# Reordering the last third of a prologue: rims, exps, table load and the third gate group of an attention and gated-FFN kernel

## The chip, the cores and the metric

The kernel runs on one core of a Trainium2 chip. The metric is the device time of one execution in microseconds (us). One core has five engines that matter here: PE (matmuls), ACT (activations and copies), DVE (vector operations), POOL (issues the loads and does some copies) and SP (issues stores and transposing transfers). PE accumulates into PSUM, of which this kernel uses eight banks.

All runs here are recorded as fast. But some runs of some experiments have a mean granted clock (the share of full speed that PE was allowed) of 0.986 to 0.993 instead of 0.997 to 1.0.

## The reference

Attention over 4 batches, 8 heads, 768 positions and 64 dimensions. Each query sees keys nearer than 16 positions, and the maximum (keys) or mean (values) of each 32-position block. Then a gated feed-forward layer on the concatenated heads:

```
scores_l = scale * q @ k.T          # masked to |i-j| < 16
scores_s = scale * q @ blockmax(k).T + log(32)
a = softmax(concat(scores_l, scores_s))
x = a @ concat(v, blockmean(v))     # 3072 tokens x 512
out = x + sigmoid(x @ w_res) * ((gelu(x @ w_gate) * (x @ w_val)) @ w_out)
```

## The kernel before

Work goes in eight units of 384 tokens. A unit has twelve gate and value groups ("fo"): four matmuls of 384 columns for the gate, four for the value, a gelu on ACT, a product on DVE. From the second unit on, the attention of the next unit lies between the matmuls of the current one. The first unit has nothing to hide its attention behind; that is the prologue, and it is written out by hand, in program order per engine.

Terms: a *rim* is a copy of neighbouring value rows into the rows 64 to 95 of a value tile, so that one matmul covers a 64-query tile and its 16 neighbours on each side. Heads go in four pairs. `vsum_pair` is PE's block means of a pair, copied by ACT to `vblk`. `av_band` and `av_blk` multiply the probabilities with the values and with the block means; `av_blk` also normalises on DVE (`rz`, `xn`) and so gives a PSUM bank back. `xt_step` transposes x on PE and copies it to `xT`. `keep_warm` multiplies zeros; it is there for PE's clock (without the last two of these matmuls four of six runs lost the clock, e8 below).

```python
def xt_step(u, ko, st, pool, tag, copy=nc.vector.tensor_copy):
    xp = pool.tile([128, TU], BF16, tag=tag, name="xp")
    # three PE transposes into xp (cut)
    copy(st["xT"][:, ko, :], xp[:])

def gv_end(gvT, fo, g, vv):
    ge = work.tile([128, TU], F32, tag="ge", name="ge")
    nc.scalar.activation(ge[:], g[:, 0:TU], AF.Gelu)
    nc.vector.tensor_mul(gvT[:, fo, :], ge[:], vv[:, 0:TU])

def mm_tile(name):                      # four banks in turn
    return ps_mm.tile([128, 512], F32, tag="mm", name=name)

def keep_warm(n, pool=ps_s, tag="s"):   # ps_s: the two score banks
    wp = pool.tile([128, 2 if pool is ps_s else 1, 512], F32, tag=tag, name="wp")
    for _ in range(n):
        nc.tensor.matmul(wp[:, 0], warm[:, 0:128], warm[:], start=True, stop=True)

# the last third of the prologue
s_step(0, 3, st, MM2, mid=lambda: vsum_pair(1, *o_bank))
pair_rims(1)
keep_warm(1, *t_bank)
av_band(0); av_blk(0)
keep_warm(1, *t_bank)
vsum_pair(2, *t_bank)
pair_rims(2)
pair_rims(3, nc.scalar.copy)
av_band(1); av_blk(1)
keep_warm(1)
vsum_pair(3, *o_bank)
# (cut: pair 2, a warming matmul, transposes and pair 3 in turn, one more warming matmul)
nc.scalar.activation(gate1[:], bias_t[0:1, :], AF.Gelu)   # brings the table load forward
# (cut: gates of groups 0 and 1 slice by slice, values behind them)
```

The softmax here doesn't subtract the row's maximum and nothing guards it: scores larger than these inputs give would overflow.

Of the kernel before, what the change touches and what calls it, by code (L numbers as in the profile page):

```python
# [8 lines left out]
F32 = mybir.dt.float32  # L9
BF16 = mybir.dt.bfloat16  # L10
AF = mybir.ActivationFunctionType
# [4 lines left out]
def kernel(  # L16
# [11 lines left out]
    nc = tc.nc  # L28
    B, H, S, D = q.shape
# [9 lines left out]
    QT = 64  # L39
# [99 lines left out]
    with tc.manual_schedule():  # L139
# [39 lines left out]
        load_q(0, q_sb[0], 1, 2)  # L179
        v_loads(0)  # L180
        load_w(w_gate, wg_src, 0)
        for x in (vext[0], vext[1][:, 0:HT]):
            pad = x[0:QT, :, :, D + 1:VP]
            nc.scalar.activation(pad, warm[0:QT, 0:1].unsqueeze(1).unsqueeze(1).to_broadcast(list(pad.shape)), AF.Copy)
        nc.vector.memset(band[:], 0.0)
# [11 lines left out]
                                    scalar1=-1.0, scalar2=240000.0, op0=ALU.add, op1=ALU.mult)  # L197
        kw_consts(0)
        nc.vector.memset(vblk[96:128, :, D:D + 1], 1.0)
        nc.vector.memset(vext[1][0:QT, HT:NT, :, D + 1:VP], 0.0)  # L200

        for c in range(6):
            if c:
# [70 lines left out]
        def pair_rims(hp, copy=nc.vector.tensor_copy):  # L274
            own_rims(0, HT, False, slice(2 * hp, 2 * hp + 2), copy)
            own_rims(0, HT, True, slice(2 * hp, 2 * hp + 2), copy)

        def vsum_pair(hp, pool, tag):
            vs = pool.tile([128, 512], F32, tag=tag, name="vs")
            hs = slice(2 * hp, 2 * hp + 2)  # L280
            for t in range(NT):
                nc.tensor.matmul(vs[:, 0:2 * D], bmat[:, t:t + 4, :], vext[0][0:QT, t, hs, 0:D],  # L282
                                 start=(t == 0), stop=(t == NT - 1))
            nc.scalar.copy(vblk[96:128, hs, 0:D], vs[96:128, 0:2 * D].rearrange("p (h d) -> p h d", d=D))
# [34 lines left out]
                                     start=(u > 0), stop=True,  # L319
                                     skip_group_check=True)  # L320

        def s_step(u, hp, st, banks=None, tiles=None, mid=None):
            if tiles:
                s, banks = tiles, True
            elif banks:
                s = [p.tile([128, 512], F32, tag=tag, name="s") for p, tag in banks]
            else:
                s2 = ps_s.tile([128, 2, 512], F32, tag="s", name="s")
                s = [s2[:, hh] for hh in range(2)]
            s_mm(u, hp, [x[:, 0:TU] for x in s])  # L330
            if mid:
                mid()
            P = ppool.tile([128, 2, HT, QT], BF16, tag="P", name="P")
            if banks:
                for hh in range(2):
                    nc.scalar.activation(P[:, hh].rearrange("p t q -> p (t q)"), s[hh][:, 0:TU], AF.Exp,  # L336
                                         scale=scale, bias=bias_t[:])
            else:
                nc.scalar.activation(P.rearrange("p a t q -> p a (t q)"), s2[:, :, 0:TU], AF.Exp,  # L339
                                     scale=scale, bias=bias_t[:])  # L340
            if u:
                Pf = P.rearrange("p a t q -> p (a t) q")
                nc.vector.tensor_mul(Pf, Pf, maskt.unsqueeze(1).to_broadcast([128, 2 * HT, QT]))  # L343
            st["P", hp] = P
# [34 lines left out]
        def xt_step(u, ko, st, pool, tag, copy=nc.vector.tensor_copy):  # L379
            xp = pool.tile([128, TU], BF16, tag=tag, name="xp")  # L380
            for sub in range(NSUB):
                nc.tensor.transpose(xp[:, sub * 128:(sub + 1) * 128],  # L382
                                    st["xn"][:, ko, sub, :], ident[:])
            copy(st["xT"][:, ko, :], xp[:])  # L384
# [20 lines left out]
        def mm_tile(name):  # L405
            return ps_mm.tile([128, 512], F32, tag="mm", name=name)
# [67 lines left out]
        def keep_warm(n, pool=ps_s, tag="s"):  # L474
# [3 lines that stand above are left out]
# [18 lines left out]
        def ao_tile(hp):  # L496
            ao[hp] = ps_mm.tile([128, NSUB, 2, D + 1], F32, tag="mm", name="ao")

        def av_band(hp):
            av_first(hp, st, ao[hp], 0, BAND)  # L500

        def av_blk(hp):
            av_first(hp, st, ao[hp], BAND, 128)
            av_end(hp, st, ao[hp])
# [12 lines left out]
        s_step(0, 2, st)  # L517
        keep_warm(2, *o_bank)
        pair_rims(0)
        s_step(0, 3, st, MM2, mid=lambda: vsum_pair(1, *o_bank))  # L520
        pair_rims(1)
        keep_warm(1, *t_bank)
        av_band(0)
        av_blk(0)
        keep_warm(1, *t_bank)
        vsum_pair(2, *t_bank)
        pair_rims(2)
        pair_rims(3, nc.scalar.copy)
        av_band(1)
        av_blk(1)  # L530
        keep_warm(1)
        vsum_pair(3, *o_bank)
        ao_tile(2)
        ao_tile(3)
        av_band(2)
        av_blk(2)
        keep_warm(1)
        xt_step(0, 0, st, **t_turn)
        av_band(3)
        av_blk(3)  # L540
        keep_warm(1)
        xt_step(0, 1, st, **t_turn)
        nc.scalar.activation(gate1[:], bias_t[0:1, :], AF.Gelu)
        g0, v0, g1 = mm_tile("g"), mm_tile("vv"), mm_tile("g")
        gv_mm(g0, w_gate, st, 0, (0, 1))
        xt_step(0, 2, st, ps_o, "ao")
        gv_mm(g1, w_gate, st, 1, (0, 1))
        gv_mm(g0, w_gate, st, 0, (2,))
        gv_mm(g1, w_gate, st, 1, (2,))
        xt_step(0, 3, st, ps_t, "t")  # L550
        gv_mm(v0, w_val, st, 0, (0, 1, 2))
        v1 = mm_tile("vv")
        gv_mm(v1, w_val, st, 1, (0, 1, 2))
        gv_mm(g0, w_gate, st, 0, (3,))
        gv_mm(v0, w_val, st, 0, (3,))
        gv_end(gvT, 0, g0, v0)
        gv_mm(g1, w_gate, st, 1, (3,))
        gv_mm(v1, w_val, st, 1, (3,))
        gv_end(gvT, 1, g1, v1)

        def unit0_extras(fo):
            if fo == 2:
# [89 lines left out]
        for u in range(NU):  # L652
            b, half = u // 2, u % 2
            nb = b + 1
            if half == 0 and nb == 1:
                k_sb[nb] = k_tile()
                load_k(nb, k_sb[nb], 0, 1)
                v_loads(nb)
                load_q_nat(nb)
            if u:  # L660
                gvT = upool.tile([128, FO, TU], BF16, tag="gvT", name="gvT")
            for fo in range(0 if u else 2, FO):
                if u > 1 and fo == 0:
                    fo_first(st, gvT)
                elif u and fo == FO - 2:
                    fo_last_two(st, gvT)
                elif u == 0 or fo < FO - 2:
                    fo_step(st, gvT, fo)
                if u == 0:
                    unit0_extras(fo)  # L670
                if u == 0 and fo == 9:
                    tq = turn_all(q_sb[1])
                if u == 0 and fo in (9, 10):
                    for hp in range(2 * fo - 18, 2 * fo - 16):
                        q_place(1, hp, tq[hp])
                if half == 0 and 1 < nb < B and fo == 0:
                    pool_after(st["xT"][0:1, KO - 1, 0:1])
                    k_nat = load_k_nat(nb)
                    v_loads(nb)
                if half == 0 and b and fo == 1:  # L680
                    v_rims(b, HT, NT)
                if half == 0 and 1 < nb < B and fo == 6:
                    turn_k(nb, k_nat)
                    k_rims(nb, slice(0, NP), nc.gpsimd)
                if half == 1 and nb < B:
                    if fo == 0:
                        v_rims(nb, 0, HT)
                        if nb > 1:
                            pool_after(st["xT"][0:1, KO - 1, 0:1])
                            load_q_nat(nb)  # L690
                    if fo == (5 if nb == 1 else 1):
                        turn_q(nb, 0)
                        turn_q(nb, 1)
                        vsum_grp(nb, ps_t, "t")
                        for i in range(2):
                            vsum_bc(nb, 3 * i, 3 * i + 3, nc.gpsimd)
                    if nb == 1:
                        if fo == 0:
                            tk = turn_all(k_sb[nb])
                        if fo in (0, 2, 4, 6):  # L700
                            hp = (2, 0, 1, 3)[fo // 2]
                            k_place(nb, hp, tk[hp])
                    elif 2 <= fo < 2 + NP:
                        k_blocks(nb, fo - 2)
            if u == NU - 1:
                last_out(u, st, gvT)
            else:
                nst = new_unit()
                (mid_out if u else first_out)(u, st, gvT, nst)
                st = nst  # L710
# [30 lines left out]
```

## Time and profile before

| | before |
|---|---|
| time | 258.07 us median of 4 runs (257.75 to 258.23) |
| span in the profile | 256.1 us |
| PE busy | 247.7 us, 97% |
| last score step starts | 14.63 us |
| third gate group starts | 25.74 us, 11.11 us later |

The difference in the last row, from the first matmul of the last score step to the first of the third gate group, is my ruler below: it contains all that the change does except the split of the pads, which comes earlier, and it is free of the scatter of the other 230 us. The prediction shows the lines on which it rests. Two more from the page of the profile, first its head, then the granted clock in tenths over 40 slices of the span:

```profile
span 256.1 us, 5856 instructions
...
PEclk9999999999999999999999999999999999999999
```

From the timeline (start, length, engine, line, operation): the last score step, the first rim copy of pair 2 on DVE and both of pair 3 on ACT.

```profile
14.63 0.34 PE L310 MATMUL s<-ident,mneg 64*128 64x384 bf16 x2
...
17.60 0.40 DVE L272 COPY vext<-vext 32x640 bf16<-32x640 bf16 x1
...
18.27 0.72 ACT L272 COPY vext<-vext 32x640 bf16<-32x640 bf16 x1
...
19.02 0.83 ACT L269 COPY vext<-vext 16x768 bf16<-16x768 bf16 x1
```

DVE copies pair 2's rims behind the first normalisation (17.01 to 17.57), and ACT is taken by pair 3's rims until 19.85. With those on it, ACT has no idle stretch as long as the 1.28 us of the gelu table between 16.13 and the load at 22.40; its longest is 0.80.

### The profile page before, as it was taken

Reading aid. Unit: us, or ns where it says so; the run is one execution under the profiler, and the core shown is the slowest. Engines: PE = TensorE matmul, PEld = TensorE weight load, DVE = VectorE, ACT = ScalarE, POOL = GpSimd, SP = SyncE. Lnnn points to the kernel's source line nnn. Section 1 sums busy time; section 2 is a strip of 40 time slices with the busy share of each in tenths; the row PEclk is TensorE's granted clock in tenths of the full one; section 3 lists DMA queues with packets and bytes.
Section 4 is the critical chain, followed back from the end, with each engine's and each line's share of the span. In section 5 each row is a group of like instructions: output and inputs, shape, how many; then the busy total and the mean of one; then the engine's idle time right before and its main releaser. Section 6 shows DMA issues by size and latency. Waiting matters only on the chain.

```text
span 256.1 us, 5856 instructions
## 1 busy us (share of the span) xinstructions
PE 247.7 (97%) x2306; PEld 140.0 (55%) x2331; DVE 158.5 (62%) x364; ACT 129.6 (51%) x216; POOL 96.9 (38%) x128
## 2 busy tenths in 40 slices
PE   7999999999999999999999999999999999999994
PEld 2675565565654565545654555546554565556544
DVE  6984785489567544867667544767567544854424
ACT  8775449355583337344493338344482338253320
POOL 8885452360705980255405980365404000000000
PEclk9999999999999999999999999999999999999999
DMA  5999999999403999279603999579703400240003
GB/s 80 176 181 196 197 204 207 174 168 184 99 4 84 192 148 171 43 137 180 125 5 100 177 152 151 67 132 174 127 17 95 117 3 0 48 140 0 4 0 123
DMA packets 98107, 29.34 MB, mean 115 GB/s; under 512 B 83224, under 2 KB 94944, under 8 KB 97984
## 3 DMA queue, kind: packets, MB, share of 16 engines
q0 software_dynamic: 68352, 14.76, 66.3%
q1 hardware_dynamic: 29728, 14.21, 24.7%
q8 instruction: 18, 0.29, 0.5%
q14 instruction: 9, 0.07, 0.1%
HBM read 29.36 MB, written 6.29 MB: 139 GB/s over the span
## 4 chain that ended last, share of the span: by engine, by line
PE 92%; DVE 5%; issue 2%; ACT 0%; DVEq 0%
PE g L397 25%; PE vv L397 24%; PE f L445 23%; PE r L435 8%; PE s L317 3%; PE ao L357 3%; PE vs L282 1%; PE tp L220 1%; PE ao L369 1%; PE vs L290 1%; PE wp L477 1%; DVE ks L237 1%; DVE o L454 1%; DVE th L451 1%; PE xp L382 1%
## 5 line engine op out<-in xcount | busy, mean ns | idle before, releaser
L403 DVE TENSOR_TENSOR gvT<-ge,vv 128x384 bf16<-128x384 f32 x96 | 52.7, 552 | 49.2 <-PE vv L397 45.3
L402 ACT ACTIVATE ge<-g 128x384 f32<-128x384 f32 x96 | 46.9, 490 | 69.2 <-DVE gvT L403 35.6
L397 PE MATMUL g<-xT,w_gate 128*128 128x384 bf16 x384 | 78.6, 326 | 0.6 <-ACT xT L384 0.4
L397 PE MATMUL vv<-xT,w_val 128*128 128x384 bf16 x384 | 78.1, 326 | 0.0
L445 PE MATMUL f<-w_out,gvT 128*128 128x512 bf16 x262 | 62.7, 379 | 1.5 <-issue 1.1
L397 PEld LDWEIGHTS <-w_gate 128*128 128x128 bf16 x384 | 37.0, 98 | 26.6 <-issue 1.9
L397 PEld LDWEIGHTS <-w_val 128*128 128x128 bf16 x384 | 37.5, 98 | 24.7
L445 PEld LDWEIGHTS <-gvT 128*128 128x128 bf16 x276 | 25.7, 98 | 29.5
L107 POOL DMA_DIRECT2D vext<-in_v_dram x32 | 24.4, 786 | 15.3 <-DMA w_out<-in_moe_w_out_dram 5.7
L438 ACT ACTIVATE th<-r 128x512 f32<-128x512 f32 x24 | 13.5, 606 | 27.5 <-PE r L435 27.5
L451 DVE SCALAR_TENSOR_TENSOR th<-th,f 128x512 f32<-128x512 f32 (+2 forms) x26 | 16.6, 640 | 14.3 <-PE f L445 14.3
L435 PE MATMUL r<-w_res,xT 128*128 128x512 bf16 x88 | 22.7, 380 | 0.4
L343 DVE TENSOR_TENSOR P<-P,maskt 128x768 bf16<-128x768 bf16 x28 | 16.1, 577 | 10.5 <-ACT P L339 6.1
L302 POOL COPY vext<-vsum 32x1536 bf16<-32x1536 bf16 x12 | 17.2, 1463 | 11.5 <-DMA vsum<-vpart 11.3
L454 DVE SCALAR_TENSOR_TENSOR o<-th,xn 128x512 f32<-128x512 f32 (+2 forms) x26 | 18.2, 700 | 0.9
L377 DVE TENSOR_TENSOR xn<-ao,rz 128x384 bf16<-128x384 f32 x32 | 17.8, 558 | 1.4 <-DVE rz L375 0.4
L339 ACT ACTIVATE P<-s,bias_t 128x768 bf16<-128x768 f32 x17 | 15.3, 901 | 4.5 <-PE s L317 4.3
L127 POOL DMA_DIRECT2D q_nat<-in_q_dram x18 | 15.8, 905 | 0.8 <-issue 0.8
L336 ACT ACTIVATE P<-s,bias_t 128x384 bf16<-128x384 f32 x30 | 15.7, 579 | 0.0
L237 DVE TENSOR_REDUCE ks<-kW 128x24 bf16<-128x768 bf16 x16 | 15.1, 941 | 0.0
L435 PEld LDWEIGHTS <-xT 128*128 128x128 bf16 x96 | 8.8, 98 | 9.9
L375 DVE RECIPROCAL rz<-ao 128x6 f32<-128x6 f32 x32 | 6.1, 191 | 12.2 <-PE ao L357 10.3
(88 smaller groups left out, 185.1 us busy)
## 6 DMA issues: line engine op xcount, KB each, us to landing
out_dram<-o SPq DMA_DIRECT2D x23, 256.0 KB, 2.2
vext<-in_v_dram POOLq DMA_DIRECT2D x32, 96.0 KB, 6.6
q_nat<-in_q_dram POOLq DMA_DIRECT2D x18, 128.0 KB, 6.2
w_gate<-in_moe_w_gate_dram POOLq DMA_DIRECT2D x6, 256.0 KB, 8.8
w_val<-in_moe_w_val_dram POOLq DMA_DIRECT2D x6, 256.0 KB, 9.0
w_out<-in_moe_w_out_dram POOLq DMA_DIRECT2D x3, 512.0 KB, 14.1
k_nat<-in_k_dram POOLq DMA_DIRECT2D x16, 96.0 KB, 5.7
vext<-vext SPq DMA_DIRECT2D x6, 144.0 KB, 4.7
```

What stands on the lines that cost most here:

```text
L107: nc.gpsimd.dma_start(out=vext[b % 2][0:QT, :, h, 0:D], in_=v[b, h].rearrange("(t p) d -> p t d", p=QT))
L237: nc.vector.tensor_reduce(out=ks.rearrange("d (t n) -> d t n", n=2), in_=kw[:, :, 0:QT].rearrange("d t (n w) -> d t n w", w=BLK), axis=myb ...
L302: eng.tensor_copy(vext[b % 2][96:128, lo:hi, :, 0:D], src)
L343: nc.vector.tensor_mul(Pf, Pf, maskt.unsqueeze(1).to_broadcast([128, 2 * HT, QT]))
L377: nc.vector.tensor_mul(xn, ao[:, :, :, 0:D], rz.to_broadcast([128, NSUB, 2, D]))
L397: nc.tensor.matmul(ps[:, 0:TU], w[:, ko, fo * 128:(fo + 1) * 128], st["xT"][:, ko, :], start=(ko == 0), stop=(ko == KO - 1), skip_group_ch ...
L402: nc.scalar.activation(ge[:], g[:, 0:TU], AF.Gelu)
L403: nc.vector.tensor_mul(gvT[:, fo, :], ge[:], vv[:, 0:TU])
L435: nc.tensor.matmul(r[:], st["xT"][:, ko, ss], w_res[:, ko, :], start=(ko == 0), stop=(ko == KO - 1))
L445: nc.tensor.matmul(st["f", sub][:], gvT[:, fo, ss], w_out[:, fo, :], start=(fo == 0), stop=(fo == FO - 1), skip_group_check=True)
L451: nc.vector.scalar_tensor_tensor(th[:, cs], th[:, cs], 1.0, f[:, 0:n], ALU.add, ALU.mult)
L454: nc.vector.scalar_tensor_tensor(o.rearrange("p (k d) -> p k d", d=128), th[:, cs].rearrange("p (k d) -> p k d", d=128), 0.5, x, ALU.mult, ...
```

## The change

It wants PE to go from the scores to the feed-forward matmuls without holes. Rims of pair 2 come ahead of the first x, those of pair 3 go from ACT to DVE, the last two exps come ahead of block mean 1, the gelu table is loaded behind block mean 2, all four copies of xT go to ACT, values are multiplied beside gates, the third group uses the score banks, and three warming matmuls go (five become two). Of a memset of pads ACT takes eight tiles instead of six and DVE the rest. The core of the diff:

```diff
-        s_step(0, 3, st, MM2, mid=lambda: vsum_pair(1, *o_bank))
+        s_step(0, 3, st, MM2)
         pair_rims(1)
-        keep_warm(1, *t_bank)
+        vsum_pair(1, *o_bank)
+        pair_rims(2)
         av_band(0)
         av_blk(0)
         keep_warm(1, *t_bank)
         vsum_pair(2, *t_bank)
-        pair_rims(2)
-        pair_rims(3, nc.scalar.copy)
+        nc.scalar.activation(gate1[:], bias_t[0:1, :], AF.Gelu)
         av_band(1)
         av_blk(1)
-        keep_warm(1)
-        vsum_pair(3, *o_bank)
         ao_tile(2)
         ao_tile(3)
+        pair_rims(3)
+        keep_warm(1)
         av_band(2)
         av_blk(2)
-        keep_warm(1)
+        vsum_pair(3, *o_bank)
+        o_turn = dict(pool=ps_o, tag="ao", copy=nc.scalar.copy)
         xt_step(0, 0, st, **t_turn)
         av_band(3)
+        xt_step(0, 1, st, **o_turn)
         av_blk(3)
-        keep_warm(1)
-        xt_step(0, 1, st, **t_turn)
# (cut: the old order of the gate and value matmuls)
+        gv_part(0, 0)                  # gate and value of one k slice
+        xt_step(0, 2, st, **t_turn)
+        gv_part(0, 1)
+        gv_mm(gv[1][0], w_gate, st, 1, (0, 1))
+        xt_step(0, 3, st, **o_turn)
+        gv_part(0, 2)
+        gv_mm(gv[1][1], w_val, st, 1, (0, 1))
+        gv_part(0, 3)
+        gv_end(gvT, 0, *gv[0])
+        gv_part(1, 2)
+        gv_part(1, 3)
+        gv_end(gvT, 1, *gv[1])
+        s2 = ps_s.tile([128, 2, 512], F32, tag="s", name="gv")
+        gv_mm(s2[:, 0], w_gate, st, 2, range(KO))
+        gv_mm(s2[:, 1], w_val, st, 2, range(KO))
+        gv_end(gvT, 2, s2[:, 0], s2[:, 1])
```

More of the change, by code (lines that the diff above doesn't have):

```diff
@@ L181 @@
         load_w(w_gate, wg_src, 0)
-        for x in (vext[0], vext[1][:, 0:HT]):
+        for x in (vext[0], vext[1][:, 0:8]):
             pad = x[0:QT, :, :, D + 1:VP]
@@ L199 @@
         nc.vector.memset(vblk[96:128, :, D:D + 1], 1.0)
-        nc.vector.memset(vext[1][0:QT, HT:NT, :, D + 1:VP], 0.0)
+        nc.vector.memset(vext[1][0:QT, 8:NT, :, D + 1:VP], 0.0)
         for c in range(6):
@@ L320, in s_mm, with s_step @@
                                      skip_group_check=True)
-        def s_step(u, hp, st, banks=None, tiles=None, mid=None):
+        def s_step(u, hp, st, banks=None, tiles=None):
             if tiles:
@@ L330, in s_step @@
             s_mm(u, hp, [x[:, 0:TU] for x in s])
-            if mid:
-                mid()
             P = ppool.tile([128, 2, HT, QT], BF16, tag="P", name="P")
@@ L526, with gv_part @@
         vsum_pair(2, *t_bank)
-        pair_rims(2)
-        pair_rims(3, nc.scalar.copy)
+        nc.scalar.activation(gate1[:], bias_t[0:1, :], AF.Gelu)
         av_band(1)
         av_blk(1)
-        keep_warm(1)
-        vsum_pair(3, *o_bank)
         ao_tile(2)
         ao_tile(3)
+        pair_rims(3)
+        keep_warm(1)
         av_band(2)
         av_blk(2)
-        keep_warm(1)
+        vsum_pair(3, *o_bank)
+        o_turn = dict(pool=ps_o, tag="ao", copy=nc.scalar.copy)
         xt_step(0, 0, st, **t_turn)
         av_band(3)
+        xt_step(0, 1, st, **o_turn)
         av_blk(3)
-        keep_warm(1)
-        xt_step(0, 1, st, **t_turn)
-        nc.scalar.activation(gate1[:], bias_t[0:1, :], AF.Gelu)
-        g0, v0, g1 = mm_tile("g"), mm_tile("vv"), mm_tile("g")
-        gv_mm(g0, w_gate, st, 0, (0, 1))
-        xt_step(0, 2, st, ps_o, "ao")
-        gv_mm(g1, w_gate, st, 1, (0, 1))
-        gv_mm(g0, w_gate, st, 0, (2,))
-        gv_mm(g1, w_gate, st, 1, (2,))
-        xt_step(0, 3, st, ps_t, "t")
-        gv_mm(v0, w_val, st, 0, (0, 1, 2))
-        v1 = mm_tile("vv")
-        gv_mm(v1, w_val, st, 1, (0, 1, 2))
-        gv_mm(g0, w_gate, st, 0, (3,))
-        gv_mm(v0, w_val, st, 0, (3,))
-        gv_end(gvT, 0, g0, v0)
-        gv_mm(g1, w_gate, st, 1, (3,))
-        gv_mm(v1, w_val, st, 1, (3,))
-        gv_end(gvT, 1, g1, v1)
+        gv = [[mm_tile("g"), mm_tile("vv")], [mm_tile("g"), mm_tile("vv")]]
+        def gv_part(fo, ko):
+            gv_mm(gv[fo][0], w_gate, st, fo, (ko,))
+            gv_mm(gv[fo][1], w_val, st, fo, (ko,))
+        gv_part(0, 0)
[14 more added lines that the diff above has]
+        gv_end(gvT, 2, s2[:, 0], s2[:, 1])
         def unit0_extras(fo):
@@ L662 @@
             for fo in range(0 if u else 2, FO):
+                if u == 0 and fo == 2:
+                    unit0_extras(fo)
+                    continue
                 if u > 1 and fo == 0:
```

## The prediction

> **What bounds the kernel now.** I read the page first, then the chain that ended last, then a table of busy time by stretch, then the timeline of the first 45 us, and last the landing times of the weight transfers.
>
> ```profile
> PE 247.7 (97%) x2306; PEld 140.0 (55%) x2331; DVE 158.5 (62%) x364; ACT 129.6 (51%) x216; POOL 96.9 (38%) x128
> ...
> PE 92%; DVE 5%; issue 2%; ACT 0%; DVEq 0%
> ```
>
> PE is busy 97% of the span and makes 92% of the chain that ended last. A busy PE is not a PE that does only needed work, so I looked for the stretches where it idles or multiplies zeros to stay warm. The change touches the prologue from the last score step on (14.63 us) to the third gate group (25.74 us), so I cut there:
>
> ```profile
> 14.63:21.70 7.07, 6.76 (x157) 5.30 (x158) 4.94 (x13) 4.57 (x9) 4.93 (x8) 1.00 1.56 193
> 21.70:25.74 4.04, 3.42 (x26) 1.89 (x23) 1.24 (x4) 2.51 (x5) 2.63 (x4) 1.00 1.45 196
> 25.74:39.79 14.05, 14.05 (x113) 8.44 (x112) 11.06 (x38) 6.88 (x16) 6.27 (x8) 1.00 1.36 202
> ```
>
> The columns are the stretch, its length, then busy PE, PEld, DVE, ACT, POOL, the granted clock, DMA share and GB/s. From 25.74 us PE is busy for all of the 14.05 us: what comes later is set by PE alone, so whatever brings the third group forward brings the end forward by as much, unless a transfer is late. The stretch before it is where time can be had:
>
> ```profile
> 20.20 0.39 PE L477 MATMUL wp<-warm 128*128 128x512 bf16 x1
> ...
> 21.31 0.39 PE L477 MATMUL wp<-warm 128*128 128x512 bf16 x1
> ...
> 21.70 0.33 PE L397 MATMUL g<-xT,w_gate 128*128 128x384 bf16 x1
> 21.90 0.48 ACT L384 COPY xT<-xp 128x384 bf16<-128x384 bf16 x1 [0.63 <-PE xp L382]
> 22.40 1.28 ACT L543 ACT_TABLE_LOAD   x1
> 22.43 0.32 PE L397 MATMUL g<-xT,w_gate 128*128 128x384 bf16 x1 [0.40 <-ACT xT L384]
> ...
> 22.96 0.36 DVE L384 COPY xT<-xp 128x384 bf16<-128x384 bf16 x1 [0.76 <-PE xp L382]
> 23.37 0.10 PEld L397 LDWEIGHTS <-w_gate 128*128 128x128 bf16 x1 [0.35 <-issue]
> ...
> 25.20 0.87 ACT L402 ACTIVATE ge<-g 128x384 f32<-128x384 f32 x2 [1.30 <-PE g L397]
> 25.74 0.81 PE L397 MATMUL g<-xT,w_gate 128*128 128x384 bf16 x4
> ```
>
> The reader is to see three holes in PE. Later in this stretch a gate or value matmul takes 0.16 us of PE (0.65 us for four in the chain). The first gate matmul at 21.70 is done with PE at 21.87, the next starts at 22.43, when ACT's second xT is there: 0.56 us. Two gate matmuls more and a transpose group end near 23.08, and the next starts at 23.37, behind DVE's xT: 0.29 us. The twelfth to sixteenth end near 25.48, and the third group starts at 25.74, 0.04 us after the first gelu (25.20, 0.50 long) has given its bank back: 0.26 us. Together 1.1 us. Besides, five warming matmuls lie between 15.73 and 21.53.
>
> [...] the first warming matmuls stand 0.42 us apart (weights at 1.60, 2.03, 2.45), those at 7.32 take 1.25 us for five. [...] The trace has the 1.28 us, and the tiny gelu behind it starts at 23.69, at once[...]. [...] the hole at 25.48 is a case of four banks for two groups of two.
>
> **The change part by part.** *Warming matmuls:* the order of instructions on PE shows three fewer, five before and two after in this part. By start-to-start times the five cost 0.32 (15.73), 0.45 (16.67), 0.32 (18.49), 0.23 (20.20) and 0.22 us (21.31). The one ahead of the third block mean stays with its 0.45, and one moves ahead of pair 2 (about 0.3). Gone: 1.54 - 0.75 = 0.8 us.
>
> *Third group in the score banks:* it needs no bank from the first gelu. The 0.26 us goes whole.
>
> *Values beside gates, copies on ACT:* each k slice now feeds two or three matmuls, with the transpose of a later slice between, so there is work while a copy runs. This should take most of 0.56 + 0.29 us. Copies two and three go from DVE (0.36) to ACT (0.48 each); ACT has room once the table load is early.
>
> *Table load:* from 22.40, between the copies, to just behind the third block mean's copy. It takes 1.28 + 0.20 us there, in a stretch where ACT owes nothing but the fourth block mean's copy.
>
> *Rims:* pair 2's copies (0.40 + 0.71 on DVE) move ahead of the first normalisation; pair 3's go from ACT (0.72 + 0.83) to DVE behind the second one.
>
> *Pad memset:* 8 tiles instead of 6 on ACT, so DVE's 1.30 us falls by a third, 0.43 us, and ACT's grows by 0.42 us, in a hole (it ended near 6.04, the next ACT work starts at 7.08). But scores start at 10.98, behind ACT's copy of qT (10.46 to 10.90), not behind DVE. I book nothing.
>
> *Replay.* PE step by step, each cost the start-to-start time of the same step in the trace before: scores 14.63 (0.34), block mean 1 14.97 (0.76), pair 0 15.73 (0.62), warm 16.35 (0.45), block mean 2 16.80 (0.76), pair 1 17.56 (0.61), warm 18.17 (0.3), pair 2 18.47 (0.62), block mean 3 19.09 (0.77), first transposes 19.86 (0.26), first half of pair 3 20.12, second transposes 20.43 (0.17), other half of pair 3 20.60 to 20.91. Then sixteen gate and value matmuls (2.6) and two transpose groups (0.34): 20.91 + 2.94 = 23.85 for the third group, if nothing waits.
>
> Now who can make it wait. DVE: pair 1's rims end at 16.01; pair 2's need the v head that was issued at 8.65 and took 7.4 us, so 16.05[...], and 1.1 us: 17.4. First normalisation (0.20 + 0.56) to 18.25: its bank goes to pair 2, which starts at 18.47, a margin of 0.2. Second to 19.05; pair 3's rims to 20.2, while PE wants them at 20.12: a wait of 0.1. Third normalisation to 21.0, fourth to 22.0, wanted near 21.3 and 22.1. ACT: exps to 16.4, block mean 1 to 16.7, block mean 2 to 17.9, table and gelu to 19.4, block mean 3 to 20.2, then the copies of xT at 20.2, 20.7, 21.6 and 22.4, each 0.48. PE wants these at 20.95, 21.45, 22.2 and 22.9. The last two come within 0.1 us. So I expect 0.1 to 0.4 us of small waits: the third group starts at 24.0 to 24.25, against 25.74. The gain is 1.5 to 1.75 us; I take 1.65.
>
> **The rivals.** *A late weight.* The first value matmul comes at 20.9 instead of 23.86, and its chunk was issued at 12.48 and took 6.8 us: 19.3. Later the tightest are the last value chunk (23.64 + 11.1 = 34.7, wanted at 35.9 after), w_res (24.96 + 12.3 = 37.3, wanted at 38.5) and the first third of w_out (26.36 + 13.5 = 39.9, wanted at 41.1). All keep about 1.2 us. If one were late by what I don't see, the gain would shrink to some 0.5 us: 257.5 us. For it speaks that the DMA share stays full over this whole stretch; against it that no matmul of before waits for a weight.
>
> *DVE becomes the bound of the prologue.* It now takes pair 3's rims as well, in one line with the normalisations, with margins of 0.1 to 0.2 us. The rim copies scatter (0.35 to 0.43, and 0.71 for the same shape). Two slow copies cost 0.7 us on the third and fourth x: a gain of 1.0, 257.0 us.
>
> *Everything fits.* No wait at all makes 1.9 us, 256.2 us. *The gain is given back later:* if the stage after 25.74 had a limit beside PE, the end would not move, 258 us; a full PE there and in the chain speaks against it.
>
> **Range and chances.** From 258.06: 258.06 - 1.65 = 256.4 us. The good end is 1.9 us plus 0.3 of scatter between runs, 255.9; the bad end is the DVE rival, 257.0, with 0.2 us more: 257.2. Faster by over 2% would need 5.2 us, more than all holes and warming matmuls of the stretch[...]. Chances: 0.01 faster, 0.98 the same, 0.01 slower.
>
> **What would show it.** In the profile after, the third gate group should start near 24.1 us and the page's last gate matmul chain keep its 0.65 us per four. Right if: three warming matmuls fewer, no PE wait for the first gelu, the fourth xT copied by ACT near 22.9, pair 3's band matmuls waiting at most 0.2 us for DVE. Wrong if: PE waits over 0.3 us for pair 3's rims or for the third or fourth x (the DVE rival), a matmul waits for a w_gate, w_val, w_res or w_out transfer (the weights), or the third group is early and the first score step of the next unit (39.79 now) is not. A matmul of 384 columns that stands 0.32 us from the next instead of 0.16 would show the clock lost.

The replay comes to 23.85 us for the third group, 24.0 to 24.25 with waits, and 1.65 us of gain. In the paragraph on waits one term is cut, an estimate of 0.2 us until DVE sees the v head: 17.4 was 16.05 + 0.2 + 1.1 and comes to 17.15 without it. What follows on DVE there was reckoned with it; the waits of 0.1 to 0.4 us and the 1.65 stand as they were recorded. (In the trace before, POOL's next issue starts at 16.34, 0.3 us behind that landing; DVE's own delay is not shown.) That the clock would stay was forecast too. The 0.32 us by which a lost clock was to be known was measured afterwards, in e8.

## The result

| | before | after |
|---|---|---|
| time, median | 258.07 us (4 runs) | 256.35 us (4 runs, 256.31 to 256.86) |
| span in the profile | 256.1 us | 254.6 us |
| last score step | 14.63 us | 14.56 us |
| third gate group | 25.74 us | 24.00 us |
| the one to the other | 11.11 us | 9.44 us |

The ratio is 0.9939 (95% interval 0.9922 to 0.9957). A ratio is the mean time of one kernel's fast runs over that of the other's of the same rounds, so it is not quite the ratio of the medians. The prediction was right: 256.4 us predicted, 256.35 measured, 1.65 us of gain foreseen, 1.72 found, and the ruler says 1.67. The four runs of the changed kernel span 0.55 us, so the last 0.05 of the agreement is luck.

The page of the profile after, its head, the busy times and the chain that ended last:

```profile
span 254.6 us, 5847 instructions
...
PE 246.6 (97%) x2303; PEld 139.7 (55%) x2328; DVE 159.4 (63%) x364; ACT 129.6 (51%) x216; POOL 97.3 (38%) x128
...
PE 93%; DVE 5%; issue 2%; DVEq 0%
```

PE did 1.1 us less and the span is 1.5 us shorter: PE's share of the chain rose. The table by stretch, with the columns of the prediction's:

```profile
21.70:24.00 2.30, 2.30 (x17) 1.38 (x16) 0.26 (x2) 1.43 (x3) 1.50 (x2) 1.00 1.45 196
24.00:39.79 15.79, 15.74 (x144) 9.43 (x143) 13.09 (x41) 8.69 (x17) 6.99 (x9) 1.00 1.37 201
```

The stretch that had 3.42 us of work in 4.04 us now has 2.30 in 2.30. The timeline, with the start of the ruler and then the same place:

```profile
14.56 0.34 PE L310 MATMUL s<-ident,mneg 64*128 64x384 bf16 x2
...
20.20 1.05 ACT L382 COPY xT<-xp 128x384 bf16<-128x384 bf16 x2
...
20.98 0.34 PE L395 MATMUL g<-xT,w_gate 128*128 128x384 bf16 x1
...
21.68 0.48 ACT L382 COPY xT<-xp 128x384 bf16<-128x384 bf16 x1 [0.43 <-PE xp L380]
...
22.50 0.48 ACT L382 COPY xT<-xp 128x384 bf16<-128x384 bf16 x1 [0.34 <-PE xp L380]
...
23.03 0.32 PE L395 MATMUL g<-xT,w_gate 128*128 128x384 bf16 x1
...
23.39 0.49 ACT L400 ACTIVATE ge<-g 128x384 f32<-128x384 f32 x1 [0.41 <-PE g L395]
...
23.84 0.33 PE L395 MATMUL vv<-xT,w_val 128*128 128x384 bf16 x1
...
24.00 0.81 PE L395 MATMUL gv<-xT,w_gate 128*128 128x384 bf16 x4
```

The reader is to see that the waits moved off PE. ACT now waits for PE's transposes (0.43 and 0.34) instead of PE for ACT. One small wait is left: three value matmuls start at 22.46 and take 0.49, so the next could start at 22.95; it starts at 23.03, right behind the fourth copy (22.50 + 0.48 = 22.98). Against my replay (23.85 - 14.63 = 9.22) the ruler is 0.22 longer: 0.08 for this wait, 0.10 because the second transposes cost 0.27 and not 0.17 when half of pair 3 follows them, 0.04 in small pieces.

### The profile page after: what moved, and what is told of

Same layout as the page of the kernel before. It is cut to its first block, busy times and chain, and to the rows that moved or that the text cites. A ratio compares the mean times of both kernels' runs of the same rounds, so it can differ in the third digit from the quotient of the medians.

```text
span 254.6 us, 5847 instructions
## 1 busy us (share of the span) xinstructions
PE 246.6 (97%) x2303; PEld 139.7 (55%) x2328; DVE 159.4 (63%) x364; ACT 129.6 (51%) x216; POOL 97.3 (38%) x128
## 4 chain that ended last, share of the span: by engine, by line
PE 93%; DVE 5%; issue 2%; DVEq 0%
PE g L395 25%; PE vv L395 24%; PE f L443 23%; PE r L433 8%; PE s L317 3%; PE ao L355 3%; PE vs L282 1%; PE ao L367 1%; PE tp L220 1%; PE vs L290 1%; DVE ks L237 1%; PE xp L380 1%; DVE o L452 1%; DVE th L449 1%; PE gv L395 1%
## 5 line engine op out<-in xcount | busy, mean ns | idle before, releaser
L395 PEld LDWEIGHTS <-w_gate 128*128 128x128 bf16 x384 | 37.1, 98 | 26.2 <-issue 1.4
```

The lines of the kernel that those rows point to most:

```text
L395: nc.tensor.matmul(ps[:, 0:TU], w[:, ko, fo * 128:(fo + 1) * 128], st["xT"][:, ko, :], start=(ko == 0), stop=(ko == KO - 1), skip_group_ch ...
```

## The experiments

All ran with the kernel before beside them, and all gave a correct result. The call with e0, e5, e7 and e8 had another chip than the other two, so times of different calls are compared through the kernel before. "Ruler" is the distance above from the profile of that run. Times in one table first:

| run | ruler, us | time, median (range), runs | clock lost in |
|---|---|---|---|
| the kernel before | 11.11 (first profile) | 257.97 to 258.10 (257.72 to 259.08), 33 | 0 |
| e0_changed_again | 9.44 | 256.63 (256.26 to 257.51), 6 | 0 |
| e1_mm_banks | 9.66 | 256.71 (256.51 to 257.05), 6 | 0 |
| e2_before_score_banks | 10.86 | 258.19 (257.69 to 258.54), 6 | 0 |
| e3_before_less_warm | 10.36 | 257.24 (257.08 to 257.41), 6 | 0 |
| e4_more_warm | 10.20 | 257.17 (257.01 to 257.86), 6 | 0 |
| e5_late_table | 10.24 | 257.28 (257.08 to 259.92), 6 | 1 |
| e6_dve_copies | 9.50 | 256.43 (256.16 to 257.43), 6 | 0 |
| e7_three_undone | 9.66 | 256.81 (256.32 to 259.56), 6 | 2 |
| e8_no_warm | clock lost | 258.08 (256.10 to 259.58), 6 | 4 |
| e9_one_warm_less | clock lost | 257.70 (256.31 to 260.07), 6 | 3 |
| e10_best_try | 9.27 | 256.13 (256.07 to 256.13), 5 | 0 |
| e11_warm_in_hole | clock lost | 257.20 (256.16 to 259.87), 6 | 2 |

"Clock lost" counts runs whose mean granted clock is under 0.995. The ratios to the kernel before mix them in for e5, e7, e8, e9 and e11, so I don't argue from those.

**The changed kernel again** (no edit).

> The changed kernel itself, so that its parts are compared on one chip. 256.3 to 256.7 us; 9.44 us from the last score step to the third gate group, within 0.1. In four earlier traces the part behind the third group took 230.4 to 230.6 us and in two 231.3: there PE waited 0.3 and 0.6 us near 182 us for a bank, behind a DVE copy that took 1.3 and 1.5 us instead of 0.23 [...]. I expect the same scatter of under 1 us here.

9.44 us again. Ratio 0.9946 (0.9928 to 0.9963). Its runs scatter over 1.25 us with no lost clock; the bank wait behind a DVE copy, suspected in the expectation, is not in the profiled run, which was a good one. It is in four of the 14 traces (e2, e4, e6 and e8), where PE waited 0.32 to 0.57 us; in e2, e4 and e6 one DVE copy had taken 1.52, 1.27 and 1.45 us instead of 0.24. e6 below shows it.

**Third group back in the rotating banks.**

```diff
-        s2 = ps_s.tile([128, 2, 512], F32, tag="s", name="gv")
-        gv_mm(s2[:, 0], w_gate, st, 2, range(KO))
-        gv_mm(s2[:, 1], w_val, st, 2, range(KO))
-        gv_end(gvT, 2, s2[:, 0], s2[:, 1])
+        fo_step(st, gvT, 2)
```

> The changed kernel with its third gate group back in the four rotating banks. Measure: from the first matmul of the last score step to the first of the third group, 11.11 us in the trace before, 9.44 after. The prediction's step (the score banks save the 0.26 us wait for the first gelu) says 9.70 and some 0.26 us more in time. Rival: once values are multiplied beside gates, group 0 ends four matmuls (0.65 us) before group 1, so its gelu (23.39, 0.49 long in the trace after) has given the bank back at 23.88, ahead of 24.00: then 9.44 to 9.5 and no difference in time. I lean to the rival.

The ruler shows 9.66, which looks like the prediction's 9.70. The timeline says otherwise:

```profile
23.80 0.49 ACT L400 ACTIVATE ge<-g 128x384 f32<-128x384 f32 x1 [0.41 <-PE g L395]
...
24.25 0.33 PE L395 MATMUL vv<-xT,w_val 128*128 128x384 bf16 x1
...
24.42 0.81 PE L395 MATMUL g<-xT,w_gate 128*128 128x384 bf16 x4
```

The third group starts 0.17 us after the last value matmul, which is the ordinary spacing: no wait. The first gelu gave the bank back at 24.29, before it was wanted. The 0.2 us lie elsewhere: in this run the twelve matmuls of pair 0 with the block means took 0.57 us instead of 0.37. Why, this one trace does not tell. So the rival holds: in the changed kernel the score banks bring nothing. The time agrees as far as it goes (ratio 0.9940 to the kernel before, beside 0.9946 for the changed kernel).

**The same part alone, in the kernel before.**

```diff
+        s2 = ps_s.tile([128, 2, 512], F32, tag="s", name="gv")
+        gv_mm(s2[:, 0], w_gate, st, 2, range(KO))
+        gv_mm(s2[:, 1], w_val, st, 2, range(KO))
+        gv_end(gvT, 2, s2[:, 0], s2[:, 1])
```

> The kernel before with one thing changed: its third group goes into the score banks. There both gelus come late (first at 25.20 in the trace before), so both theories of the other bank run allow that the 0.26 us wait at 25.48 goes: 10.85 us instead of 11.11, and 257.8 us. If it stays 11.11, the wait was for something other than the bank.

```profile
25.22 0.33 PE L397 MATMUL vv<-xT,w_val 128*128 128x384 bf16 x1
25.38 0.81 PE L397 MATMUL gv<-xT,w_gate 128*128 128x384 bf16 x4
```

The ruler gives 10.86: the third group now starts 0.16 us behind the last value matmul, and the wait for the bank goes, 0.25 us. So the wait was for the bank, and there are two ways to be rid of it, the score banks or an order in which group 0 ends well before group 1. The change does both, and the second makes the first superfluous. The time (ratio 0.9994, 0.9977 to 1.0011) can't show a thousandth: in the profiled run PE lost 0.57 us near 182 us, waiting for a bank.

**Three warming matmuls out of the kernel before, and three into the changed one.**

```diff
# e3, in the kernel before
-        keep_warm(1, *t_bank)
         av_band(0)
-        keep_warm(1)
         xt_step(0, 0, st, **t_turn)
-        keep_warm(1)
         xt_step(0, 1, st, **t_turn)
# e4, in the changed kernel
+        keep_warm(1, *t_bank)
         av_band(0)
+        keep_warm(1)
         xt_step(0, 0, st, **t_turn)
         av_band(3)
+        keep_warm(1)
         xt_step(0, 1, st, **o_turn)
```

> The kernel before without three of its five warming matmuls (ahead of pair 0, of the first and of the second transposes). My theory, that these cost their start-to-start time: 0.32 + 0.23 + 0.22 = 0.77 us, so 10.3 to 10.4 us and 257.3 us. Rival: they fill waits for rims and copies, which show up in their place: 10.9 to 11.1 and no gain, because the change's gain is its new order alone. A matmul of 384 columns 0.32 us from the next would show the clock lost.

> The changed kernel with three warming matmuls put back, ahead of pair 0, of the first and of the second transposes. If warming matmuls are pure cost there: 9.44 + 0.77 = 10.2 us and 257.1 us. If they would only fill waits that the new order leaves: under 9.8.

10.36 is 0.75 less than 11.11, and 10.20 is 0.76 more than 9.44. Each warming matmul costs what it takes, in either order, and nothing takes its place. The times follow: 257.24 and 257.17. This is 0.75 of the change's 1.67 us, and it needs none of the reordering. The clock was kept in all twelve runs.

**The table load late.**

```diff
         vsum_pair(2, *t_bank)
-        nc.scalar.activation(gate1[:], bias_t[0:1, :], AF.Gelu)
# (cut)
         av_blk(3)
+        nc.scalar.activation(gate1[:], bias_t[0:1, :], AF.Gelu)
```

> The changed kernel with its gelu table load behind the second copy of xT, where it was before. ACT makes all four copies now, so theory: the table and the tiny gelu (1.28 + 0.20 us from 21.25) hold the third and fourth copy back to 23.2 and 23.7, the third slice's matmuls wait 0.95 us, and the small wait for the fourth copy goes: 9.44 + 0.87 = 10.3 us and some 0.85 us more in time. Rival: the table's place is of no account, because the gelus come only at 23.4: 9.44 to 9.6.

```profile
21.23 1.28 ACT L540 ACT_TABLE_LOAD   x1
...
22.64 0.82 ACT L382 COPY xT<-xp 128x384 bf16<-128x384 bf16 x2
...
23.14 0.32 PE L395 MATMUL g<-xT,w_gate 128*128 128x384 bf16 x1 [0.71 <-ACT xT L382]
```

10.24: the table costs 0.80 us if it sits between the copies. PE waits 0.88 us for the third copy (22.26 to 23.14), and the 0.08 for the fourth goes. The theory holds, a little smaller than worked out. One of six runs lost the clock, though it has as many warming matmuls as the changed kernel.

**Two copies back on DVE.**

```diff
-        xt_step(0, 2, st, **t_turn)
+        xt_step(0, 2, st, ps_t, "t")
-        xt_step(0, 3, st, **o_turn)
+        xt_step(0, 3, st, ps_o, "ao")
```

> The changed kernel with the third and fourth copy of xT on DVE again (0.36 us instead of ACT's 0.48). The prediction counted the move to ACT among what takes the holes away. Rival: the order of PE's work does it alone. DVE is free from 21.88 on in the trace after, so its copies would end near 22.26 and 22.86, wanted at 22.30 and 22.95: the wait of 0.08 for the fourth copy goes, 9.36 us instead of 9.44, no difference in time. If the move mattered: over 9.5.

The wait for the fourth copy is gone: three value matmuls at 22.57, the next gate matmul at 23.06. The ruler reads 9.50 all the same, because in this run pair 3's rims took 0.35 + 0.61 us on DVE and ended at 20.15, so that pair 3 started at 20.20 and not 20.07. That is the scatter of the rim copies that the DVE rival spoke of, worth 0.13 us here. The move of copies to ACT was not needed; the order of PE's work was. The times agree (ratio 0.9940).

This profiled run also caught the scatter of the later units in the act. From the timeline, DVE's copies, POOL's and PE's next wait:

```profile
177.53 0.24 DVE L241 COPY kW<-ks 128x288 bf16<-128x288 bf16 x1
...
179.13 1.45 DVE L241 COPY kW<-ks 128x288 bf16<-128x288 bf16 x1
```

```profile
179.02 2.88 POOL L302 COPY vext<-vsum 32x1536 bf16<-32x1536 bf16 x2 [4.27 <-DMA vsum<-vpart]
```

```profile
181.09 0.81 PE L395 MATMUL g<-xT,w_gate 128*128 128x384 bf16 x4 [0.50 <-DVE gvT L401]
```

POOL began two copies (1.46 each) at 179.02, DVE its copy 0.11 later. DVE's ended near 180.5, when POOL's first ended: 1.45 us instead of 0.24. The products behind it came late, so did the banks, and PE lost 0.50 us. In e2 POOL began 0.04 us ahead (180.49 and 180.53) and DVE's copy took 1.52, in e4 0.29 ahead (179.82 and 180.11) and it took 1.27; in the trace after, DVE began first (179.12, POOL at 179.49) and its copy took 0.23. So the times agree; what holds DVE's copy back no view shows. POOL was ahead by only 0.11 us here, and a kernel that differs from the others only in the prologue may or may not lose that half microsecond: four of the 14 traces did.

**Three parts undone together:** pair 2's rims behind the first x, block mean 1 ahead of the exps, the old split of the pads.

```diff
-        s_step(0, 3, st, MM2)
+        s_step(0, 3, st, MM2, mid=lambda: vsum_pair(1, *o_bank))
         pair_rims(1)
-        vsum_pair(1, *o_bank)
-        pair_rims(2)
# (cut)
         vsum_pair(2, *t_bank)
+        pair_rims(2)
# (cut: pads of vext[1] split at tile 6 again instead of 8)
```

> The changed kernel with three parts undone to which I gave no gain: pair 2's rims behind the first x again, block mean 1 ahead of the last two exps again, and the pads' memset split as before. Theory: none lies on PE's path; 9.44 to 9.6 us (pair 2's matmuls want the rims at 18.43, they would end near 18.2, or 18.5 with slow copies) and no difference in time. Rival: the rims ahead of the first x are what lets pair 2 start: 9.8 us or more.

9.66, just above the range of my theory and below the rival's. Pair 2 starts 0.45 us behind the warming matmul instead of 0.32, so it waited 0.13 us for rims that ended at 18.59; the rims of pair 3 come later too and cost 0.08. So the early rims are worth about 0.2 us in this trace; I had booked nothing. That the two other parts are worth nothing is not shown apart. Two of six runs lost the clock.

**No warming matmuls in this part.**

```diff
-        keep_warm(1, *t_bank)
         vsum_pair(2, *t_bank)
# (cut)
-        keep_warm(1)
         av_band(2)
```

> The changed kernel without the last two warming matmuls of this part as well. Theory: PE sets the pace there and DVE and ACT keep up. By replay with the trace after, pair 2 waits under 0.1 us for its bank and the fourth xT 0.1 us: 8.7 to 8.8 us instead of 9.44, and 0.65 to 0.7 us off the time, near 255.7. Rival: DVE's rims of pair 3 and the copies take the place of the warming matmuls: 9.2 us or more. A lost clock would show as 384 columns every 0.32 us.

The two runs with a full clock took 256.10 and 256.18 us; the four others 257.67 to 259.58. The expected 255.7 us is missed even by the two: the profiled run, a lost one, has a wait of 0.45 us for pair 3's rims, whose first copy took 0.70 us instead of 0.35, and no kept run was profiled. From the table by stretch of the profiled run:

```profile
15.98:19.39 3.41, 3.41 (x95) 2.85 (x88) 2.90 (x8) 2.48 (x6) 3.03 (x4) 1.00 1.46 196
```

```profile
19.30:19.40 0.10, 0.10 (x3) 0.03 (x1) 0.10 (x1) 0.10 (x1) 0.00 (x0) 0.92 1.50 205
19.40:19.50 0.10, 0.04 (x1) 0.09 (x1) 0.07 (x2) 0.08 (x2) 0.02 (x1) 0.50 1.39 189
...
26.20:26.30 0.10, 0.10 (x3) 0.01 (x1) 0.10 (x1) 0.00 (x0) 0.07 (x1) 0.95 1.43 195
```

```profile
19.88 0.54 PE L367 MATMUL ao<-vext,P 96*64 96x65 bf16 x12 [0.45 <-DVE vext L269]
...
22.19 0.53 PE L395 MATMUL g<-xT,w_gate 128*128 128x384 bf16 x1
...
22.51 0.53 PE L395 MATMUL vv<-xT,w_val 128*128 128x384 bf16 x1
```

The clock (third number from the end) falls to a half at 19.38. In the 3.41 us before it PE shows busy 3.41 of 3.41 us, and its first hole, the 0.45 us wait for pair 3's rims, comes afterwards. So the profile shows no hole in the 3.41 us before the fall; since it models the ends of matmuls (one of 384 columns is shown 0.33 us long where the next starts after 0.16), gaps under some 0.15 us would not show. At half clock a 384-column matmul stands 0.32 us from the next instead of 0.16, and the clock is back only at 26.2, 6.8 us later. The stretch in question holds block means, matmuls of 64 output rows by 65 columns and the first transposes, and no warming matmul. What takes the clock is not shown.

**One warming matmul less.**

```diff
-        keep_warm(1)
         av_band(2)
```

> The changed kernel without the warming matmul ahead of pair 2 alone. In runs that keep the clock: 9.44 - 0.3 + up to 0.1 of waiting for pair 3's rims, 9.15 to 9.25 us. Theory from the run without both[...] (it went at 19.38, behind a window in which PE showed busy for 3.41 of 3.41 us and ahead of the first hole), so with one warming matmul fewer some of six runs, but fewer than four, lose it (mean clock 0.987, 259.3 to 259.9 us). [...]

Three of six runs lost it (258.91, 259.28 and 260.07), three kept it (256.31 to 256.50). The profiled run lost it at 19.42 us, with no hole in the 3.4 us before: the view shows 0.38 us of idle time ahead of block mean 2, but there the kernel has its other warming matmul, whose record is missing, as in the trace of the changed kernel. Three of six lies within what I expected (some, but fewer than four).

**Two warming matmuls where PE waits anyway.**

```diff
# on top of e8
         xt_step(0, 0, st, **t_turn)
+        keep_warm(2)
         av_band(3)
```

> The kernel without the last two warming matmuls, with two new ones where PE waited 0.45 us for pair 3's rims there, ahead of pair 3's first half. In runs that keep the clock the two lie in that wait: 9.0 to 9.15 us and 256.0 us. Theory [...]: the stretch from 16 to 19.1 us stays as thin as in the run without both, so runs [...] still lose the clock, if fewer than four of six. [...]

Two of six lost the clock (258.87, 259.87); in the profiled run it went at 18.70, ahead of the new matmuls. Four kept it: 256.16, 256.28, 256.87 and 257.53. The free place is too late for runs in which it goes before.

**A better version, from all this.**

```diff
-        keep_warm(1, *t_bank)
+        keep_warm(1)
         vsum_pair(2, *t_bank)
# (cut: third and fourth copy of xT on DVE, as in e6)
                     elif 2 <= fo < 2 + NP:
                         k_blocks(nb, fo - 2)
+                        if fo == 1 + NP:
+                            pool_after(kW[nb % 2][0:1, 0, NP - 1, BAND:BAND + 1])
+                            for i in range(2):
+                                vsum_bc(nb, 3 * i, 3 * i + 3, nc.gpsimd)
# (and these two copies taken out of their old place for nb > 1)
```

> A try for a better version, from what the runs showed; as many warming matmuls as in the changed kernel. The one ahead of block mean 2 goes to another bank than block mean 2 (start to start 0.45 now, 0.3 then), the third and fourth copy of xT go to DVE, and POOL's copies of block means in the later units wait until DVE is through with its key blocks. Expected: 9.44 - 0.13 - 0.08 = 9.2 to 9.25 us; no DVE copy of 0.23 us that takes over 0.6 near 135 and 180 us and no wait of PE for a bank there, so less scatter; 256.1 us in the middle, all runs within 0.5 us; no lost clock.

The ruler gives 9.27: the warming matmul in another bank than the block mean behind it costs 0.32 instead of 0.45 from start to start (16.27 to 16.59), and the wait for the fourth copy is gone. And the scatter is gone: five runs within 0.06 us, 256.13 in the middle, ratio 0.9921 (0.9909 to 0.9933), all with the clock kept. DVE's last key copy and POOL's copies in its profile:

```profile
178.81 0.23 DVE L241 COPY kW<-ks 128x288 bf16<-128x288 bf16 x1
```

```profile
179.41 2.88 POOL L302 COPY vext<-vsum 32x1536 bf16<-32x1536 bf16 x2
```

POOL waits for DVE's copy on purpose, so these two cannot overlap (POOL's begin at 179.41, DVE's ends at 179.04). That this order, of the three edits, took the scatter away is likely and not shown apart: e6 has the copies on DVE without it and scatters over 1.27 us, but the move of the warming matmul was not tried alone. This version is faster than the kernel before by 0.8%. Its five runs also lie below all ten of the changed kernel (the lowest is 256.26). They were run at other times.

## Why the prediction was right

The total was right to 0.05 us, which is better than runs repeat; the mechanism was PE's start-to-start times plus the holes. The 0.22 us above the replay lie in the 0.1 to 0.4 that the prediction allowed for waits, but only 0.08 of it is a wait: the second transposes had been taken at 0.17 us and cost 0.27. The steps stand as follows.

- *Three warming matmuls, 0.8 us.* Right: 0.75 and 0.76 measured, out of one kernel and into the other.
- *PE alone sets what comes after.* Right: the first score step of the next unit came 1.6 us earlier (38.22 for 39.86 in the chain), as did all later stages, and no weight was late.
- *"The 0.26 us goes whole" with the score banks.* Right that it goes, wrong in why. In the kernel before, the banks alone do it (0.25). In the changed one they are superfluous, because the values beside the gates end group 0 earlier. I had added up two parts of which either would have been enough; the sum came out right because I counted the hole once.
- *Values beside gates and copies on ACT, most of 0.85 us.* Right in size. The holes of 0.56 and 0.29 became a single wait of 0.08, foreseen as "within 0.1". But the copies on ACT did not do it: with two of them back on DVE the wait is gone. What is left is the order of PE's work, by exclusion; it was not undone by itself.
- *The table load early.* Right: late, it costs 0.80.
- *Rims: nothing booked.* The size was off: with the two other undone parts, about 0.2 us. The DVE rival, with its margins of 0.1 to 0.2, was the right place to look: 0.13 us in e6 and in e7.
- *Pads.* Booked as nothing. The last score step starts 0.07 us earlier in the profile after, but other runs with the old split have it at 14.52 to 14.65, so this is scatter.
- *The clock should stay*. It stayed in all ten runs of the changed kernel. But it fell where the profile shows no hole: at 19.38 us in e8, behind 3.41 us in which PE shows busy for 3.41. And one warming matmul fewer lost it in three of six runs (e9). Of the variants with as many as the changed kernel, e5 and e7 lost it in three of twelve runs, e1, e6 and e10 in none of 17. So that the change itself kept it in ten runs is in part luck.

What stays open: what takes the clock. A PE that shows busy does not keep it (3.41 of 3.41 us in e8), and with fewer warming matmuls of 128 by 512 it was lost more often: in four of six runs without the last two (e8), in three of six without one (e9), in three of 39 with both in place (the changed kernel, e1, e5, e6, e7 and e10).

## What to carry to other kernels

Where an engine sets the pace, write its stream down from start-to-start times and check each neighbour against it: the sum was good to 0.22 us of 9.44. When two parts of a change remove the same wait, count it once, and undo them one at a time if you want to know which one to keep. Warming matmuls have a price that shows in every run (0.25 us each in e3 and e4) and a use that shows only in some (three of six in e9), so judge their removal by the clock of six runs, not by the profile of one.
